# 26 products on zeros for TensorE in three of its waits at the start of a recurrent-attention and maxout kernel

## The chip, the cores and the metric

The kernel runs on one core of a Trainium2 chip. The metric is the device time in microseconds (us) of one execution; the time of a kernel is the median over its runs.

## The reference

The inputs are q, k, v and f_logit, each 4 batches x 8 heads x 768 positions x 48, and the three weight matrices of a maxout layer. All are float32, and so is the output of 3072 x 384.

```python
f = 1.0 / (1.0 + np.exp(-f_logit))
for t in range(S):
    state = f[:, :, t, :, None] * state + np.einsum('bhd,bhe->bhde', k[:, :, t], v[:, :, t])
    y[:, :, t] = np.einsum('bhd,bhde->bhe', q[:, :, t], state)
x = y.transpose(0, 2, 1, 3).reshape(B * S, H * D)
h1, h2 = x @ w1, x @ w2
out = np.maximum(h1, h2) @ w_out
```

## The kernel before

The 768 positions of each of the 4 batches are cut into windows of 256, so that there are 12 units of work, numbered 0 to 11 (unit s is window s // 4 of batch s % 4). The positions of a window are taken in chunks, and the recurrence becomes a few products per chunk. The maxout layer is rewritten: max(h1, h2) is h2 plus the ReLU of x @ (w1 - w2), so the kernel first makes the difference of the two weight matrices and the product of w2 and w_out, and then needs one wide product, one ReLU and one product with w_out for each unit.

The order of all work is written out by hand in a string, ORDER. Each word is a step: letters for the kind, the unit, for some steps a part, the engine (a = ScalarE, v = VectorE, p = GpSimd, s = SyncE) and after @ a slot of the input buffer or a bank of PSUM. An engine runs its own steps in the order in which they stand in the string; waits between engines are put in by the framework from the buffers that the steps read and write. All loads and nearly all stores go through the one DMA queue of SyncE.

The steps of the opening that matter here:

- Lf, Lk, Lq, Lv load a unit's f_logit, k, q and v into slots of one large buffer (line 115); Wa, Wb and Wo load w1, w2 (line 125) and w_out (line 129), in halves.
- E, F, G (lines 246, 250, 254) take exponentials and a logarithm of f_logit on ScalarE; e (line 257) adds two of its rows.
- C (lines 261 and 264) is the running sum over the chunk as a product with a triangular matrix, u_inc; X and Z (lines 271 and 276) take its exponentials.
- i, j, K, Q (lines 280 to 294) scale k and q; V casts v.
- t and u (line 320) transpose k and q on TensorE; U copies the transposes out of PSUM (tile trs).
- D (line 401) adds up the new state; n and N scale it. A (line 337) is the product of queries and keys, m (line 345) its mask, S (line 367) the part from the state before, y (line 387) the product with the values. z reads a word of a PSUM bank, H and Y (line 433) gather the result as xT.
- wc, wt, wx cast, transpose and store w2; ws (line 536) subtracts w2 from w1, wp (line 544) permutes the difference, we stores it; wo casts w_out, and wm (line 528) multiplies the two, wn stores that.
- d (line 445), r (line 452), o (lines 460 and 463), b and O are the layer itself: the wide product, its ReLU, the last product, the copy out of PSUM and the store.

TensorE's own order at the start is C0, t0, D0, u0, the two parts of A0, S0, C1, then products for the weights, y0 and the first d0. PSUM has eight banks; bank 7 is first used by the weight step wt1.

Of the kernel before, what the change touches and what calls it, by code (L numbers as in the profile page):

```python
# [12 lines left out]
BF16 = mybir.dt.bfloat16  # L13
# [4 lines left out]


ORDER = """  # L20
Lf0s@12 Lk0s@13 Lq0s@14 Lv0s@15 E0a Wb0s F0a Lf1s@12 G0a i0v Wb1s e0v C0@0 Wa0s X0a Wa1s Z0a K0v
V0p j0v t0@0 Lq1s@13 D0@2 Q0v Lv1s@15 n0.0v u0@0 E1a n0.1v U0v@0 F1a e1p A0.0@0 wc1a A0.1@2
m0.0v@0 S0@4 G1a Lk1s@12 wc0a C1@6 z0v@4 wt1@7 ws1v wc2a m0.1v@2 wp1@0 wx1a@7 ws3v y0 Z1a Wo0s
ws0v we1a@0 wp3@2 H0a@4 ws2v wt2@7 we3a@2 Wo1s wp0@0 j1v X1a wp2@2 Y0v@4 Q1p we0a@0 Lf2s@0 wt0@6
wx2a@7 we2v@2 d0.0@0 d0.1@1 i1v V1a K1v d0.2@2 Lf4s@13 r0.0a@0 u1@4 wx0v@6 t1@4 wo1p d0.3@3 U1v@4
wo0p D1@0 r0.1a@2 Lq2s@9 n1.0v A1.0@6 A1.1@4 wo3a wo2v S1@2 n1.1v Lk2s@10 m1.0v@6 wm0@0 E2a z1v@2
m1.1v@4 Lv2s@11 wm2@1 F2a E4a e2p y1 Lk4s@0 F4a C2@4 H1v@2 wm1@5 Y1v@2 Z2a e4p G2a Lq4s@13 wn0a@0
C4@6 X2a d1.0@2 i2v wn2a@1 j2v wn1a@5 d1.1@3 Lf3s@8 Z4a Q2v d1.2@0 X4a G4a K2v d1.3@1 V2a Lf5s@9
u2@4 t2@4 r1.1a@0 i4v o0.0@6 U2v@4 K4p Lv4s@11 r1.0a@2 j4v A2.0@0 b0.0a@6 Lq3s@10 D2@2 N1.1p
o0.1@4 n2.0v E3a m2.0v@0 Q4p Lv3s@0 F3a n2.1v S2@0 b0.1a@4 A2.1@2 z2v@0 E5a t4@6 N0.1p m2.1v@2  # L30
Lk3s@13 u4@6 N2.1p o1.0@5 F5a U4v@6 V4a Lf6s@9 e5v G5a y2 j3v b1.0a@5 D4@2 A4.0@6 H2a@0 O0s n4.0v
o1.1@5 m4.0v@6 N4.0p Lk5s@11 V3a e3p Lv5s@8 n4.1v G3a Y2v@0 C5@6 b1.1a@5 C3@7 i3p X5a S4@2 Z3a
A4.1@4 Lq5s@0 z4v@2 d2.0@0 Z5a Q3v X3a d2.1@1 E6a K3v d2.2@6 r2.0a@0 m4.1v@4 d2.3@7 Lq6s@13 t3@0
r2.1a@6 u3@0 i5p y4 D3@4 U3a@0 Lk6s@9 H4v@2 K5p o2.0@6 n3.0v Y4v@2 Lf8s@10 F6a n3.1v S3@0 b2.0v@6
A3.0@2 e6p A3.1@4 m3.0v@2 d4.0@6 Lf7s@11 N4.1p d4.1@7 j5v V5p d4.2@2 z3v@0 r4.0a@6 Lk8s@12 m3.1v@4
d4.3@3 G6a D5@6 Q5v r4.1a@2 y3 O1s C6@5 j6v H3a@0 o2.1@4 Lv6s@0 Z6a i6v E8a Y3v@0 Lq8s@8 X6a F8a
t5@2 N3.1v u5@2 b2.1v@4 Lv7s@10 d3.0@0 U5a@2 e8v d3.1@1 n5.0v Q6v d3.2@4 K6v E7a d3.3@5 Lq7s@13
C8@2 N5.0v r3.1a@4 o4.0@3 r3.0v@0 V6p F7a Lf10s@9 n5.1v G8a e7v N5.1p D6@0 Z8a A5.0@4 b4.0v@3 X8a
t6@6 Lf9s@0 j8v u6@6 C7@2 U6a@6 n6.0v o3.0@3 m5.0v@4 N6.0p Lk7s@11 V7p n6.1v X7a i8v A5.1@0
b3.0a@3 A6.0@6 S5@4 Lf11s@10 j7v Z7a K8p o3.1@3 z5v@4 m5.1v@0 Lq9s@15 m6.0v@6 y5 S6@0 Q8v H5a@4  # L40
Lv8s@12 A6.1@6 G7a o4.1@2 E9a z6v@0 i7p m6.1v@6 F9a Y5v@4 b3.1a@3 y6 e9p E10a O3s t8@6 u8@6 K7p
H6a@0 d5.0@3 Lk9s@9 U8v@6 G9a Lq10s@0 b4.1a@2 C9@5 d5.1@4 X9a O4s Y6v@0 Z9a N6.1p d5.2@6 r5.0a@3
O2s d5.3@7 Q7v d6.0@0 r5.1a@6 Lk11s@11 j9v A8.0@2 Lq11s@13 Q9p D7@4 V8a m8.0v@2 u7@6 t7@6 d6.1@1
U7a@6 n7.0v Lv9s@12 d6.2@2 N7.0v n7.1v d6.3@3 j10v E11a o5.0@4 r6.0v@0 r6.1a@2 N7.1v A7.0@0
Lv11s@10 b5.0a@4 D8@2 A7.1@6 F11a n8.0v S7@4 m7.0v@0 o6.0@3 F10a e11p Lk10s@15 G10a z7v@4 N8.0p
m7.1v@6 e10p C11@0 Lv10s@8 b6.0a@3 S8@1 i9v A8.1@6 V9p o5.1@3 z8v@1 m8.1v@6 K9v C10@6 y7 Z10a
b5.1v@3 D9@7 j11v H7a@4 y8 O5s Z11a Y7v@4 o6.1@3 X11a Q11p H8a@1 n9.0v Y8v@1 d7.0@4 b6.1a@3 i10p
G11a d7.1@5 O6s i11v d8.0@0 r7.0a@4 Q10v d8.1@1 N9.0v X10a d8.2@2 V10a K10v d8.3@3 r8.0a@0 K11v
d7.2@4 d7.3@5 r8.1v@2 u10@6 r7.1a@4 t9@0 u9@0 t10@6 t11@2 U9a@0 U10v@6 u11@2 o8.0@4 U11v@2 A9.0@0
b8.0a@4 S9@2 m9.0v@0 A9.1@6 D10@4 o7.1@5 z9v@2 m9.1v@6 V11v A11.0@0 y9 n10.0v D11@6 o7.0@4 n11.0v  # L50
m11.0v@0 N11.0p H9v@2 o8.1@0 b7.0v@4 N10.0v b7.1a@5 Y9v@2 O7s A10.0@6 b8.1a@0 S10@4 m10.0v@6
A10.1@2 d9.0@0 z10v@4 d9.1@1 m10.1v@2 d9.2@6 r9.0a@0 d9.3@7 A11.1@0 r9.1a@6 S11@2 y10 z11v@2
m11.1v@0 o9.0@6 H10a@4 Y10v@4 y11 b9.0a@6 d10.0@0 H11v@2 d10.1@1 d10.2@4 r10.0v@0 o9.1@6 Y11v@2
d10.3@5 d11.0@0 r10.1a@4 d11.1@1 b9.1a@6 d11.2@2 O9s d11.3@3 O8s o10.0@4 r11.1v@2 r11.0v@0 o10.1@3
o11.0@0 b10.0a@4 b10.1a@3 O10s P11.0@1 b11.0a@0 O11s P11.1@0 B11.0v@1 R11.0s B11.1a@0 R11.1s
"""


@with_exitstack
def kernel(  # L60
# [14 lines left out]
    nc = tc.nc  # L75
    B, H, S, D = q.shape
    C = 128
    HC = C // 2
    W = 2 * C
    nw = S // W  # L80
    NP = H // 2
# [8 lines left out]
    consts = ctx.enter_context(tc.tile_pool(name="consts", bufs=1))  # L90
    inp = ctx.enter_context(tc.tile_pool(name="inp", bufs=1))
    work = ctx.enter_context(tc.tile_pool(name="work", bufs=2))
# [16 lines left out]
    loaded = {s: {} for s in range(n_s)}  # L109
    sources = {"f": f_logit, "k": k, "q": q, "v": v}  # L110

    def load(nm, s, slot):
        w, b = divmod(s, B)
        src = sources[nm][b, :, w * W:(w + 1) * W, :].rearrange("h (p two) d -> p h (two d)", two=2)
        nc.sync.dma_start(out=slots[:, slot, :].rearrange("p (h x) -> p h x", h=H), in_=src)
        loaded[s][nm] = slots[:, slot, :].rearrange("p (h two d) -> p h two d", h=H, two=2)

    def staged(i, a):
        return slots[:, 4 * i:4 * i + 4, :].rearrange("p s x -> p (s x)").rearrange("p (a x) -> p a x", a=a)
# [10 lines left out]
                             in_=moe_w_out.rearrange("(j p) m -> p j m", p=C)[:, part, :])  # L130


    tri = consts.tile([C, 2, HC], BF16, name="tri")
    nc.gpsimd.memset(tri, 0.0)
    for h in range(2):
# [27 lines left out]
    def pad(nm, s):  # L163
        if s not in holders[nm]:
            holders[nm].append(s)
        return padded[nm][holders[nm].index(s) % len(padded[nm])]
# [157 lines left out]
    def step_U(s, e, b):  # L324
        t = work.tile([C, 2, 2, NP, 2, HC], BF16, name="trs", tag="trs", bufs=3)
        copy(e, t.rearrange("p h x j a t -> p h (x j a t)"), banks16[:, b:b + 2, :])
        tr[s] = t

    def step_A(s, jj, b):
        t = tr[s]  # L330
        for j in range(2 * jj, 2 * jj + 2):
            for par in range(2):
                for h in range(2):
                    for r in range(2):
                        rows = slice(r * DP, r * DP + D)
                        ps = banks[:, b + r, :].rearrange("p (j a t) -> p j a t", j=2, a=2)
                        nc.tensor.matmul(out=ps[h * HC:(h + 1) * HC, j % 2, par, :],  # L337
                                         lhsT=t[rows, h, 0, j, par, :],
                                         rhs=t[rows, h, 1, j].rearrange("p a t -> p (a t)"),
                                         start=True, stop=True, skip_group_check=True)  # L340

    def step_m(s, jj, b):
        if jj == 0:
            at[s] = work.tile([C, 2, 2, 2, 2, C], BF16, name="at_m", tag="at_m", bufs=2)
        nc.vector.tensor_mul(at[s][:, jj].rearrange("p r j a t -> p (r j) (a t)"),  # L345
                             banks[:, b:b + 2, :].rearrange("p r (j x) -> p (r j) x", j=2),
                             mask_f.unsqueeze(1).to_broadcast([C, 4, 2 * C]))
# [9 lines left out]
    def step_S(s, b):  # L357
        t = tr[s]
        ys[s] = [banks[:, b + h, :].rearrange("p (j t) -> p j t", j=NP) for h in range(2)]
        for h in range(2):  # L360
            if not has_state(s, h):
                continue
            st = state_before(s, h)
            for j in range(NP):
                for r in range(2):
                    rows = slice(r * DP, r * DP + D)
                    nc.tensor.matmul(  # L367
                        out=ys[s][h][r * DP:(r + 1) * DP, j, :], lhsT=st[rows, j, :],
                        rhs=t[rows, h, 1, j].rearrange("p a t -> p (a t)"),
                        start=(j == 0), stop=False, skip_group_check=True)  # L370


# [176 lines left out]
    def store_wd(part, e, b):  # L549
        n = d_ff // 4  # L550
        ps = banks[:, b:b + 2, :].rearrange("p b x -> p (b x)")[:, 0:KT * n]
        copy(e, wd[:, :, part * n:(part + 1) * n], ps.rearrange("p (k x) -> p k x", k=KT))

    steps = {
        "Lf": lambda s, e, b: load("f", s, b), "Lk": lambda s, e, b: load("k", s, b),
        "Lq": lambda s, e, b: load("q", s, b), "Lv": lambda s, e, b: load("v", s, b),
        "Wa": lambda i, e, b: load_columns(w1_f, moe_w1, e, i),
        "Wb": lambda i, e, b: load_columns(w2_f, moe_w2, e, i),
        "Wo": lambda h, e, b: load_wo(e, h),
# [5 lines left out]
        "V": lambda s, e, b: step_V(s, e),  # L565
        "t": lambda s, e, b: transposes(s, 0, b), "u": lambda s, e, b: transposes(s, 1, b),
        "U": lambda s, e, b: step_U(s, e, b),
        "A": lambda s, i, e, b: step_A(s, i, b), "m": lambda s, i, e, b: step_m(s, i, b),
        "S": lambda s, e, b: step_S(s, b), "y": lambda s, e, b: step_y(s),
        "z": lambda s, e, b: step_z(s, b),  # L570
# [10 lines left out]
        "ws": lambda i, e, b: subtract(i, e), "wp": lambda i, e, b: permuted(i, b),  # L581
        "we": lambda i, e, b: store_wd(i, e, b),
    }
    for word in ORDER.split():
        key, of, e, b = re.fullmatch(r"([A-Za-z]+)([0-9.]+)([avps]?)@?([0-9]*)", word).groups()
        steps[key](*map(int, of.split(".")), e, int(b or 0))


# [28 lines left out]
```

## Time and profile before

| | |
|---|---|
| median of 3 runs | 141.44 us (141.24 to 141.84) |
| the profiled execution, its own time | 142.99 us |
| its span, first to last instruction | 141.2 us |
| TensorE products busy | 120.8 us (86% of the span), 2331 instructions |
| VectorE busy | 110.4 us (78%) |
| ScalarE busy | 87.2 us (62%) |
| GpSimd busy | 47.7 us (34%) |
| SyncE's DMA queue | 28.22 MB, 80.9% of what 16 DMA engines could be busy in the span |

How to read it: times in the profile count from the start of the span, 1.8 us of the profiled execution lie around it. PE is TensorE's products, PEld its loading of the stationary operand, DVE VectorE, ACT ScalarE, POOL GpSimd, SPq SyncE's DMA queue. In a row of the timeline stand the start, the time that the merged instructions took, the engine, the line, the operation, what is written and read, how many there are, and in brackets how long the engine had been idle and what ended that. Products overlap in TensorE's pipeline, so the duration of one is longer than the distance between two. A row of the chain of waits has the start, the length, and the engine or transfer that held the chain.

### The profile page before, as it was taken

How to read it: one execution, taken by the hardware profiler on the slowest of the kernel's cores; microseconds unless marked ns; L12 is line 12 of the kernel's file. 1: busy time of each engine (PE TensorE's matmuls, PEld its weight loads, DVE VectorE, ACT ScalarE, POOL GpSimd, SP SyncE). 2: the span in 40 equal slices, each digit the busy share in tenths (PEclk: the TensorE clock that was granted, in tenths of full speed). 3: DMA queues.
4: the chain of work that ended last, by engine and by line, in shares of the span. 5: the costliest groups of instructions: out<-in, count | busy, mean ns of one | idle time of the engine just before them, and what ended most of it. 6: DMA issues, size and time to landing. Idle time of an engine off the chain costs nothing.

```text
span 141.2 us, 5372 instructions
## 1 busy us (share of the span) xinstructions
PE 120.8 (86%) x2331; PEld 89.9 (64%) x2331; DVE 110.4 (78%) x196; ACT 87.2 (62%) x145; POOL 47.7 (34%) x68
## 2 busy tenths in 40 slices
PE   0033899896999999999699999997999999999990
PEld 0022678653866786868466787675886668678570
DVE  5766799896879997999989898899688895770610
ACT  3624899559988899499683999715785114303120
POOL 7443205405194536800582943459100000000000
PEclk9999999999999999999999999999999999999999
DMA  4999999999999998997999999999410012000854
GB/s 114 269 331 348 382 278 300 341 236 265 264 262 269 278 276 212 248 230 185 272 265 250 233 256 271 271 271 238 101 25 5 5 34 77 5 0 16 214 125 98
DMA packets 56248, 28.66 MB, mean 203 GB/s; under 512 B 50464, under 2 KB 54688, under 8 KB 56224
## 3 DMA queue, kind: packets, MB, share of 16 engines
q1 hardware_dynamic: 56064, 28.22, 80.9%
q8 instruction: 18, 0.29, 0.9%
q10 hardware_dynamic: 160, 0.10, 0.3%
q14 instruction: 6, 0.05, 0.1%
HBM read 23.59 MB, written 4.72 MB: 200 GB/s over the span
## 4 chain that ended last, share of the span: by engine, by line
PE 57%; DMA 20%; DVE 7%; issue 5%; ACT 4%; POOL 3%; SPq 1%; ACTq 0%; DVEq 0%; POOLq 0%
PE banks L445 17%; PE banks L463 17%; DMA slots<-in_f_logit_dram 8%; PE banks L460 7%; DMA slots<-in_k_dram 6%; DMA slots<-in_moe_w_dram 6%; PE banks L337 3%; PE banks L320 3%; PE banks L387 3%; PE banks L367 2%; DVE kp L291 2%; POOL vb L104 2%; PE banks L401 2%; ACT gate L246 1%; POOL wo L104 1%
## 5 line engine op out<-in xcount | busy, mean ns | idle before, releaser
L445 PE MATMUL banks<-xT,wd 128*128 128x256 bf16 x288 | 33.7, 273 | 0.0
L463 PE MATMUL banks<-wo,gT 128*128 128x384 bf16 x184 | 33.7, 326 | 0.0
L345 DVE TENSOR_TENSOR at_m<-banks,mask 128x1024 bf16<-128x1024 f32 x24 | 29.0, 1215 | 1.7 <-PE banks L337 1.2
L445 PEld LDWEIGHTS <-wd 128*128 128x128 bf16 x288 | 27.3, 98 | 3.9
L452 ACT ACTIVATE gT<-banks 128x1024 bf16<-128x1024 f32 x18 | 18.4, 1032 | 11.8 <-PE banks L445 11.6
L463 PEld LDWEIGHTS <-gT 128*128 128x128 bf16 x184 | 18.0, 98 | 11.9
L104 ACT COPY ob<-banks 128x384 f32<-128x384 f32 (+1 forms) x19 | 8.9, 468 | 19.9 <-PE banks L463 14.8
L433 DVE SCALAR_TENSOR_TENSOR xT<-tail,gaps,banks 128x256 bf16<-128x256 bf16 x36 | 15.1, 472 | 0.1
L460 PE MATMUL banks<-m,xT 128*128 128x384 bf16 x69 | 15.1, 328 | 0.0
L246 ACT ACTIVATE gate<-slots 128x768 f32<-128x768 f32 x12 | 10.1, 846 | 7.2 <-DMA slots<-in_f_logit_dram 7.2
L104 POOL CAST vb<-slots 128x384 bf16<-128x384 f32 (+2 forms) x15 | 9.3, 657 | 13.8 <-DVE gT L454 8.3
L257 POOL TENSOR_TENSOR e<-ell 128x384 bf16<-128x384 f32 x8 | 8.0, 1001 | 13.5 <-ACT ell L250 13.5
L418 POOL TENSOR_TENSOR state<-tmp_s,dec 128x256 bf16<-128x256 f32 x10 | 6.5, 651 | 17.9 <-DVE tmp_s L413 17.9
L337 PE MATMUL banks<-trs 48*64 48x128 bf16 x384 | 10.5, 227 | 1.9 <-DVE trs L104 1.9
L261 PE MATMUL banks<-e,u_inc 128*128 128x384 bf16 x12 | 4.3, 354 | 9.2 <-DVE e L257 7.8
L454 DVE TENSOR_SCALAR gT<-banks 128x1024 bf16<-128x1024 f32 x6 | 7.2, 1218 | 4.3 <-PE banks L445 4.3
L337 PEld LDWEIGHTS <-trs 48*64 48x64 bf16 x384 | 7.5, 110 | 4.5 <-DVE trs L104 2.2
L104 ACT COPY trs<-banks 128x2048 bf16<-128x2048 bf16 x5 | 9.3, 1861 | 1.6 <-PE banks L320 1.6
L250 ACT ACTIVATE ell<-gate 128x768 f32<-128x768 f32 x12 | 10.0, 844 | 0.4
L294 POOL TENSOR_TENSOR qp<-slots,dec 128x768 bf16<-128x768 f32 x4 | 7.3, 1819 | 8.7 <-DVE slots L284 6.8
L104 DVE COPY trs<-banks 128x2048 bf16<-128x2048 bf16 x7 | 8.4, 1217 | 1.5 <-PE banks L320 1.5
L291 DVE TENSOR_TENSOR kp<-slots,inv 128x768 bf16<-128x768 f32 x8 | 7.5, 952 | 1.4 <-ACT inv L271 1.2
(73 smaller groups left out, 195.3 us busy)
## 6 DMA issues: line engine op xcount, KB each, us to landing
slots<-in_f_logit_dram SPq DMA_DIRECT2D x12, 384.0 KB, 6.4
slots<-in_k_dram SPq DMA_DIRECT2D x12, 384.0 KB, 5.7
slots<-in_q_dram SPq DMA_DIRECT2D x12, 384.0 KB, 6.0
slots<-in_v_dram SPq DMA_DIRECT2D x12, 384.0 KB, 5.9
out_dram<-ob SPq DMA_DIRECT2D x22, 192.0 KB, 3.5
slots<-in_moe_w_dram SPq DMA_DIRECT2D x4, 768.0 KB, 8.4
slots<-in_moe_w_out_dram SPq DMA_DIRECT2D x2, 768.0 KB, 7.4
out_dram<-ob SPq DMA_DIRECT2D x2, 96.0 KB, 2.2
```

Source lines behind the costliest of these rows:

```text
L104: (nc.scalar.copy if e == "a" else engines[e].tensor_copy)(out, in_)
L246: nc.scalar.activation(flat(gate[s]), flat(loaded[s]["f"]), AF.Exp, bias=0.0, scale=-1.0)
L250: nc.scalar.activation(flat(ell[s]), flat(gate[s]), AF.Ln, bias=1.0, scale=1.0)
L257: engines[e].tensor_add(pad("e", s)[:, :, 0:D], ell[s][:, :, 0, :], ell[s][:, :, 1, :])
L291: engines[e].tensor_mul(pad("kp", s)[:, :, :, 0:D], by_parity(loaded[s]["k"]), both(inv[s]))
L337: nc.tensor.matmul(out=ps[h * HC:(h + 1) * HC, j % 2, par, :], lhsT=t[rows, h, 0, j, par, :], rhs=t[rows, h, 1, j].rearrange("p a t -> p ( ...
L345: nc.vector.tensor_mul(at[s][:, jj].rearrange("p r j a t -> p (r j) (a t)"), banks[:, b:b + 2, :].rearrange("p r (j x) -> p (r j) x", j=2) ...
L433: engines[e].scalar_tensor_tensor(out=x[:, kt], in0=tails[s], scalar=gaps[:, kt:kt + 1], in1=ps[:, :, kt], op0=ALU.mult, op1=ALU.add)
L445: nc.tensor.matmul(out=ps[:, f, :], lhsT=wd[:, kt, ff * C:(ff + 1) * C], rhs=xT[g][:, kt, :], start=(kt == 0), stop=(kt == KT - 1))
L452: nc.scalar.activation(dst, src, AF.Relu)
L460: nc.tensor.matmul(out=ps, lhsT=xT[g][:, kt, cols], rhs=m2[:, kt, :], start=(kt == 0), stop=False)
L463: nc.tensor.matmul(out=ps, lhsT=gT[g][:, ff, cols], rhs=wo[:, ff, :], start=False, stop=(ff == FG - 1))
```

## The change

A tile of zeros, 128 x 512 in bf16, is set once by VectorE, ahead of its other work. A new step, J, issues a number of products of this tile with itself (a stationary operand of 128 x 128 zeros, a moving operand of 128 x 512 zeros) into PSUM bank 7. Nothing reads their result. Fifteen stand ahead of C0, six between C0 and t0, and five between u0 and A0. No step of the string is moved, removed or given to another engine.

The diff also has code that nothing calls: an empty string FIRST for loads ahead of everything, a step T that the string does not name, and an engine argument for loads, which is SyncE everywhere as before. The view of the transposed tile has its axes in another order, with the same addresses behind it.

```diff
 ORDER = """
-Lf0s@12 Lk0s@13 Lq0s@14 Lv0s@15 E0a Wb0s F0a Lf1s@12 G0a i0v Wb1s e0v C0@0 Wa0s X0a Wa1s Z0a K0v
-V0p j0v t0@0 Lq1s@13 D0@2 Q0v Lv1s@15 n0.0v u0@0 E1a n0.1v U0v@0 F1a e1p A0.0@0 wc1a A0.1@2
+Lf0s@12 Lk0s@13 Lq0s@14 Lv0s@15 J15@7 E0a Wb0s F0a Lf1s@12 G0a i0v Wb1s e0v C0@0 J6@7 Wa0s X0a
+Wa1s Z0a K0v V0p j0v t0@0 Lq1s@13 D0@2 Q0v Lv1s@15 n0.0v u0@0 J5@7 E1a n0.1v U0v@0 F1a e1p A0.0@0
...
+    idle = consts.tile([C, 512], BF16, name="idle")
+    nc.vector.memset(idle, 0.0)
     tri = consts.tile([C, 2, HC], BF16, name="tri")
...
-        tr[s] = t
+        tr[s] = t.rearrange("p h x j a t -> p x h j a t")
...
-                                         lhsT=t[rows, h, 0, j, par, :],
-                                         rhs=t[rows, h, 1, j].rearrange("p a t -> p (a t)"),
+                                         lhsT=t[rows, 0, h, j, par, :],
+                                         rhs=t[rows, 1, h, j],
...
+    def step_J(n, b):
+        for _ in range(n):
+            nc.tensor.matmul(out=banks[:, b, :], lhsT=idle[:, 0:C], rhs=idle, start=True, stop=True)
...
+        "J": lambda n, e, b: step_J(n, b),
```

More of the change, by code (lines that the diff above doesn't have):

```diff
@@ L20 @@
 ORDER = """
-Lf0s@12 Lk0s@13 Lq0s@14 Lv0s@15 E0a Wb0s F0a Lf1s@12 G0a i0v Wb1s e0v C0@0 Wa0s X0a Wa1s Z0a K0v
-V0p j0v t0@0 Lq1s@13 D0@2 Q0v Lv1s@15 n0.0v u0@0 E1a n0.1v U0v@0 F1a e1p A0.0@0 wc1a A0.1@2
[L23 to L55, printed above, removed]
-"""
+Lf0s@12 Lk0s@13 Lq0s@14 Lv0s@15 J15@7 E0a Wb0s F0a Lf1s@12 G0a i0v Wb1s e0v C0@0 J6@7 Wa0s X0a
@@ new lines @@
+Wa1s Z0a K0v V0p j0v t0@0 Lq1s@13 D0@2 Q0v Lv1s@15 n0.0v u0@0 J5@7 E1a n0.1v U0v@0 F1a e1p A0.0@0
+wc1a A0.1@2 m0.0v@0 S0@4 G1a Lk1s@12 wc0a C1@6 z0v@4 wt1@7 ws1v wc2a m0.1v@2 wp1@0 wx1a@7 ws3v y0
+Z1a Wo0s ws0v we1a@0 wp3@2 H0a@4 ws2v wt2@7 we3a@2 Wo1s wp0@0 j1v X1a wp2@2 Y0v@4 Q1p we0a@0
+Lf2s@0 wt0@6 wx2a@7 we2v@2 d0.0@0 d0.1@1 i1v V1a K1v d0.2@2 Lf4s@13 r0.0a@0 u1@4 wx0v@6 t1@4 wo1p
+d0.3@3 U1v@4 wo0p D1@0 r0.1a@2 Lq2s@9 n1.0v A1.0@6 A1.1@4 wo3a wo2v S1@2 n1.1v Lk2s@10 m1.0v@6
+wm0@0 E2a z1v@2 m1.1v@4 Lv2s@11 wm2@1 F2a E4a e2p y1 Lk4s@0 F4a C2@4 H1v@2 wm1@5 Y1v@2 Z2a e4p G2a
@@ new lines @@
+Lq4s@13 wn0a@0 C4@6 X2a d1.0@2 i2v wn2a@1 j2v wn1a@5 d1.1@3 Lf3s@8 Z4a Q2v d1.2@0 X4a G4a K2v
+d1.3@1 V2a Lf5s@9 u2@4 t2@4 r1.1a@0 i4v o0.0@6 U2v@4 K4p Lv4s@11 r1.0a@2 j4v A2.0@0 b0.0a@6
+Lq3s@10 D2@2 N1.1p o0.1@4 n2.0v E3a m2.0v@0 Q4p Lv3s@0 F3a n2.1v S2@0 b0.1a@4 A2.1@2 z2v@0 E5a
+t4@6 N0.1p m2.1v@2 Lk3s@13 u4@6 N2.1p o1.0@5 F5a U4v@6 V4a Lf6s@9 e5v G5a y2 j3v b1.0a@5 D4@2
+A4.0@6 H2a@0 O0s n4.0v o1.1@5 m4.0v@6 N4.0p Lk5s@11 V3a e3p Lv5s@8 n4.1v G3a Y2v@0 C5@6 b1.1a@5
+C3@7 i3p X5a S4@2 Z3a A4.1@4 Lq5s@0 z4v@2 d2.0@0 Z5a Q3v X3a d2.1@1 E6a K3v d2.2@6 r2.0a@0 m4.1v@4
@@ new lines @@
+d2.3@7 Lq6s@13 t3@0 r2.1a@6 u3@0 i5p y4 D3@4 U3a@0 Lk6s@9 H4v@2 K5p o2.0@6 n3.0v Y4v@2 Lf8s@10 F6a
+n3.1v S3@0 b2.0v@6 A3.0@2 e6p A3.1@4 m3.0v@2 d4.0@6 Lf7s@11 N4.1p d4.1@7 j5v V5p d4.2@2 z3v@0
+r4.0a@6 Lk8s@12 m3.1v@4 d4.3@3 G6a D5@6 Q5v r4.1a@2 y3 O1s C6@5 j6v H3a@0 o2.1@4 Lv6s@0 Z6a i6v
+E8a Y3v@0 Lq8s@8 X6a F8a t5@2 N3.1v u5@2 b2.1v@4 Lv7s@10 d3.0@0 U5a@2 e8v d3.1@1 n5.0v Q6v d3.2@4
+K6v E7a d3.3@5 Lq7s@13 C8@2 N5.0v r3.1a@4 o4.0@3 r3.0v@0 V6p F7a Lf10s@9 n5.1v G8a e7v N5.1p D6@0
+Z8a A5.0@4 b4.0v@3 X8a t6@6 Lf9s@0 j8v u6@6 C7@2 U6a@6 n6.0v o3.0@3 m5.0v@4 N6.0p Lk7s@11 V7p
@@ new lines @@
+n6.1v X7a i8v A5.1@0 b3.0a@3 A6.0@6 S5@4 Lf11s@10 j7v Z7a K8p o3.1@3 z5v@4 m5.1v@0 Lq9s@15 m6.0v@6
+y5 S6@0 Q8v H5a@4 Lv8s@12 A6.1@6 G7a o4.1@2 E9a z6v@0 i7p m6.1v@6 F9a Y5v@4 b3.1a@3 y6 e9p E10a
+O3s t8@6 u8@6 K7p H6a@0 d5.0@3 Lk9s@9 U8v@6 G9a Lq10s@0 b4.1a@2 C9@5 d5.1@4 X9a O4s Y6v@0 Z9a
+N6.1p d5.2@6 r5.0a@3 O2s d5.3@7 Q7v d6.0@0 r5.1a@6 Lk11s@11 j9v A8.0@2 Lq11s@13 Q9p D7@4 V8a
+m8.0v@2 u7@6 t7@6 d6.1@1 U7a@6 n7.0v Lv9s@12 d6.2@2 N7.0v n7.1v d6.3@3 j10v E11a o5.0@4 r6.0v@0
+r6.1a@2 N7.1v A7.0@0 Lv11s@10 b5.0a@4 D8@2 A7.1@6 F11a n8.0v S7@4 m7.0v@0 o6.0@3 F10a e11p
@@ new lines @@
+Lk10s@15 G10a z7v@4 N8.0p m7.1v@6 e10p C11@0 Lv10s@8 b6.0a@3 S8@1 i9v A8.1@6 V9p o5.1@3 z8v@1
+m8.1v@6 K9v C10@6 y7 Z10a b5.1v@3 D9@7 j11v H7a@4 y8 O5s Z11a Y7v@4 o6.1@3 X11a Q11p H8a@1 n9.0v
+Y8v@1 d7.0@4 b6.1a@3 i10p G11a d7.1@5 O6s i11v d8.0@0 r7.0a@4 Q10v d8.1@1 N9.0v X10a d8.2@2 V10a
+K10v d8.3@3 r8.0a@0 K11v d7.2@4 d7.3@5 r8.1v@2 u10@6 r7.1a@4 t9@0 u9@0 t10@6 t11@2 U9a@0 U10v@6
+u11@2 o8.0@4 U11v@2 A9.0@0 b8.0a@4 S9@2 m9.0v@0 A9.1@6 D10@4 o7.1@5 z9v@2 m9.1v@6 V11v A11.0@0 y9
+n10.0v D11@6 o7.0@4 n11.0v m11.0v@0 N11.0p H9v@2 o8.1@0 b7.0v@4 N10.0v b7.1a@5 Y9v@2 O7s A10.0@6
@@ new lines, with words @@
+b8.1a@0 S10@4 m10.0v@6 A10.1@2 d9.0@0 z10v@4 d9.1@1 m10.1v@2 d9.2@6 r9.0a@0 d9.3@7 A11.1@0 r9.1a@6
+S11@2 y10 z11v@2 m11.1v@0 o9.0@6 H10a@4 Y10v@4 y11 b9.0a@6 d10.0@0 H11v@2 d10.1@1 d10.2@4 r10.0v@0
+o9.1@6 Y11v@2 d10.3@5 d11.0@0 r10.1a@4 d11.1@1 b9.1a@6 d11.2@2 O9s d11.3@3 O8s o10.0@4 r11.1v@2
+r11.0v@0 o10.1@3 o11.0@0 b10.0a@4 b10.1a@3 O10s P11.0@1 b11.0a@0 O11s P11.1@0 B11.0v@1 R11.0s
+B11.1a@0 R11.1s
+"""
+FIRST = ""
+def words(order):
+    for word in order.split():
+        key, of, e, b = re.fullmatch(r"([A-Za-z]+)([0-9.]+)([avps]?)@?([0-9]*)", word).groups()
+        yield key, tuple(map(int, of.split("."))), e, int(b or 0)
@@ L110, with load @@
     sources = {"f": f_logit, "k": k, "q": q, "v": v}
-    def load(nm, s, slot):
+    def load(nm, s, e, slot):
         w, b = divmod(s, B)
         src = sources[nm][b, :, w * W:(w + 1) * W, :].rearrange("h (p two) d -> p h (two d)", two=2)
-        nc.sync.dma_start(out=slots[:, slot, :].rearrange("p (h x) -> p h x", h=H), in_=src)
+        engines[e].dma_start(out=slots[:, slot, :].rearrange("p (h x) -> p h x", h=H), in_=src)
         loaded[s][nm] = slots[:, slot, :].rearrange("p (h two d) -> p h two d", h=H, two=2)
+    for key, of, e, b in words(FIRST):
+        load(key[1], *of, e, b)
     def staged(i, a):
@@ L326, in step_U, with step_T @@
         copy(e, t.rearrange("p h x j a t -> p h (x j a t)"), banks16[:, b:b + 2, :])
-        tr[s] = t
+        tr[s] = t.rearrange("p h x j a t -> p x h j a t")
+    def step_T(s, x, e):
+        if s not in tr:
+            t = work.tile([C, 2, 2, NP, 2, HC], BF16, name="trs", tag="trs", bufs=3)
+            tr[s] = t.rearrange("p h x j a t -> p (h x j a t)").rearrange(
+                "p (x a j h t) -> p x h j a t", x=2, a=2, j=NP, h=2)
+        out = tr[s][:, x].rearrange("p h j a t -> p a j h t").rearrange("p a j h t -> p (a j) (h t)")
+        engines[e].dma_start_transpose(
+            out=out, in_=pad("kpqp"[2 * x:2 * x + 2], s).rearrange("p two h e -> p (two h e)"))
     def step_A(s, jj, b):
@@ L368, in step_S @@
                         out=ys[s][h][r * DP:(r + 1) * DP, j, :], lhsT=st[rows, j, :],
-                        rhs=t[rows, h, 1, j].rearrange("p a t -> p (a t)"),
+                        rhs=t[rows, 1, h, j],
                         start=(j == 0), stop=False, skip_group_check=True)
@@ L552, in store_wd @@
         copy(e, wd[:, :, part * n:(part + 1) * n], ps.rearrange("p (k x) -> p k x", k=KT))
+    def step_J(n, b):
+        for _ in range(n):
+            nc.tensor.matmul(out=banks[:, b, :], lhsT=idle[:, 0:C], rhs=idle, start=True, stop=True)
     steps = {
-        "Lf": lambda s, e, b: load("f", s, b), "Lk": lambda s, e, b: load("k", s, b),
-        "Lq": lambda s, e, b: load("q", s, b), "Lv": lambda s, e, b: load("v", s, b),
+        "J": lambda n, e, b: step_J(n, b),
+        "Lf": lambda s, e, b: load("f", s, e, b), "Lk": lambda s, e, b: load("k", s, e, b),
+        "Lq": lambda s, e, b: load("q", s, e, b), "Lv": lambda s, e, b: load("v", s, e, b),
         "Wa": lambda i, e, b: load_columns(w1_f, moe_w1, e, i),
@@ L567 @@
         "U": lambda s, e, b: step_U(s, e, b),
+        "T": lambda s, x, e, b: step_T(s, x, e),
         "A": lambda s, i, e, b: step_A(s, i, b), "m": lambda s, i, e, b: step_m(s, i, b),
@@ L583 @@
     }
-    for word in ORDER.split():
-        key, of, e, b = re.fullmatch(r"([A-Za-z]+)([0-9.]+)([avps]?)@?([0-9]*)", word).groups()
-        steps[key](*map(int, of.split(".")), e, int(b or 0))
+    for key, of, e, b in words(ORDER):
+        steps[key](*of, e, b)
 _INS = ['q', 'k', 'v', 'f_logit', 'moe_w1', 'moe_w2', 'moe_w_out']
```

## The prediction

> **What bounds the kernel now.** I read the slices of the page first. The two rows below share the span out in 40 slices of 3.5 us; a digit is the busy share in tenths.
>
> ```profile
> PE   0033899896999999999699999997999999999990
> ...
> DMA  4999999999999998997999999999410012000854
> ```
>
> The DMA engines are busy from the second slice to the 28th, about 100 us. TensorE is idle for two slices, partly busy up to some 35 us, and then nearly full to the end. So two things can set the end: the loads, and TensorE from about 35 us on. A change in the opening counts only if it moves the moment from which TensorE is full.
>
> The timeline of TensorE's products over the first 36 us shows the three waits that the change fills, and that moment.
>
> ```profile
> 7.79 0.48 PE L261 MATMUL banks<-e,u_inc 128*128 128x384 bf16 x1 [7.79 <-DVE e L257]
> 8.06 0.29 PE L264 MATMUL banks<-ones,e 128*128 128x2 bf16 x4
> 9.93 0.61 PE L320 MATMUL banks<-ident,kp 64*128 64x64 bf16 x16 [1.58 <-DVE kp L291]
> 11.92 0.65 PE L401 MATMUL banks<-vb,kp 64*64 64x64 bf16 x32 [1.38 <-POOL vb L104]
> 12.50 0.61 PE L320 MATMUL banks<-ident,qp 64*128 64x64 bf16 x16
> 14.74 1.07 PE L337 MATMUL banks<-trs 48*64 48x128 bf16 x32 [1.64 <-DVE trs L104]
> ...
> 33.32 0.32 PE L261 MATMUL banks<-e,u_inc 128*128 128x384 bf16 x1 [1.37 <-POOL e L257]
> ```
>
> J15 goes ahead of the first row, J6 between C0 (7.79, 8.06) and t0 (9.93), J5 between u0 (12.50) and A0 (14.74). The last row is C2. TensorE stood idle for 1.37 us before it; the stage table has it busy for 26.68 of the 26.70 us that follow, and the chain of waits stays on it to 53 us. So C2 is the moment. The timeline of all engines shows what holds it:
>
> ```profile
> 26.15 1.60 POOL L104 CAST wo<-slots 128x768 bf16<-128x768 f32 x2 [2.34 <-DMA slots<-in_moe_w_out_dram]
> ...
> 30.48 0.84 ACT L246 ACTIVATE gate<-slots 128x768 f32<-128x768 f32 x1 [1.39 <-DMA slots<-in_f_logit_dram]
> 31.36 0.84 ACT L250 ACTIVATE ell<-gate 128x768 f32<-128x768 f32 x1
> ...
> 32.28 0.99 POOL L257 TENSOR_TENSOR e<-ell 128x384 bf16<-128x384 f32 x1 [4.53 <-ACT ell L250]
> ```
>
> E2, F2, e2 and C2 follow one another with no slack, and E2 waited 1.39 us for its load, f2. C2 is set by a transfer, and the steps ahead of it hang on transfers too. The chain of waits, with start and length, has
>
> ```profile
> 6.28 8.15 DMA slots<-in_moe_w_dram
> ...
> 15.12 8.84 DMA slots<-in_k_dram
> ```
>
> which land at 14.43 (wc1 at 14.51 waits for it) and 23.96 (i1 at 23.98). In the trace's landing records the halves of w1 arrive at 16.45 and 18.55, q1 at 21.20, those of w_out at 26.09 and 28.24, f2 at 30.41: one stream with no hole. VectorE's ws1, ws3, j1 and i1 start at 16.64, 18.64, 21.30 and 23.98, close behind.
>
> **What the Trainium skill says.** "TensorE: Matmul & The Clock Gate", Part 1: TensorE's clock is halved until it has been busy for a window of about 3.4 us, and the window is free-running. The trace agrees on the size: 16 transposes take 0.61 us at 9.93 and 12.50, but 0.41 at 24.92; the permuting products (L544) fall from 421 to 273 ns within the group at 17.64. So the opening runs at half clock to about 18.4 us. No sentence of the page says that zeros count less for this gate than other data, and no run yet shows it. The same page, Part 2, has weight loads pulled ahead of products in flight: the trace shows u_inc loaded at 1.99 for a product at 7.79, and 0.77 us of loads inside the 1.01 us of wt1. "VectorE: DVE Perf Modes", "Zero memsets can be issued as uint32 (trn2)", halves the elements of the new memset; the trace agrees, with uint32 rows for bf16 tiles (L155 and L158).
>
> **The change part by part.**
>
> *The memset.* Four rows of 528 words take 2.17 us (L155), 0.54 each, so 256 words are some 0.26 us, at the head of VectorE's queue. Queued behind it are the memsets and copies of u_inc. The first copy waits 0.34 us for GpSimd's tri, and before i0 VectorE waits 0.82 us for ScalarE's exponential of the load f0. Cost 0; were it 0.53, the 0.82 would still cover it.
>
> *One J.* At full clock, 256 columns (L445, 18 in 2.17 us, one of them 0.27) are 0.112 us apart, 384 columns (L528, 16 in 2.77, one of them 0.33) 0.163. So 128 columns are 0.051, and 512 are 0.214; at half clock twice that, 0.43. Weight loads of 0.10 us hide behind them.
>
> *J15.* VectorE starts at 0.82; with the memset the zeros are there at about 1.1. All at half clock end at 1.15 + 15 x 0.43 = 7.6, ahead of e0's 7.79. If a full window lifts the clock, which can be at 4.6 to 8.0 by its phase, the end is as early as 1.15 + 8 x 0.43 + 7 x 0.214 = 6.1. Cost 0, with a pipeline's tail of 0.1 at worst.
>
> *J6.* C0 would end near 8.2 at full clock; 6 x 0.214 = 1.3 gives 9.5, ahead of t0's 9.9. At half clock 8.4 + 2.6 = 11.0, and t0 is 1.1 late, but D0 behind it waits for GpSimd's V0 until 11.92, so that nothing passes on. Cost 0.
>
> *J5.* At full clock u0 ends near 12.9, and 1.1 more is 14.0, ahead of A0's 14.7. At half clock it is 13.1 + 2.15 = 15.25, and A0 is 0.5 late. What waits is the mask m0, VectorE's whole queue behind it, and S0, C1 and the weight steps on TensorE. C2's 1.37 us of idle time covers that, and VectorE's wait of 0.47 us for w_out at 28.26 takes up most of it there.
>
> *The gain.* At full clock, row by row: C0 -0.16, t0, D0 and u0 -0.20 each, A0 -0.43, S0 -0.25, C1 -0.15, wt1 -0.40, the first seven L544 products -0.36: 2.35 us of TensorE's time. On a path lie only C0 (X0 waits for it), D0 (the update of the state waits 0.9 us for it) and the first half of A0 (m0 waits 0.74 us): 0.16, and 0.2 + 0.2 after V0 has set D0. So VectorE leads by 0.4 at 15.4 us. Then ws1 cannot start before 16.45, ws3 not before 18.55 (a lead of 0.09), i1 not before 23.96 (0.02). TensorE's lead, up to 2 us, becomes a longer wait before C2. No load moves: v1, k1, w_out and f2 are issued behind V0, E1 and one another, and though q1 is issued after K0 at 9.90, and could go 0.16 sooner, it stands behind the weights, the last of which lands at 18.55.
>
> *The sum.* 0 - 0 = 0 on the profiled execution of 142.99 us, whose span is 141.2. That execution is 1.55 above the median of 141.44; the difference carries over, so 141.4.
>
> **The rivals.**
>
> *A lead gets through (faster).* If C2 hung on something other than f2, or the loads came sooner with the steps that free their slots, VectorE's 0.4 us up to half of TensorE's 2 us could arrive, most likely 0.9: 140.5. The steps' starts at 16.64 to 30.48, each within 0.2 us of a landing, speak against it.
>
> *Each J serial with its weight load, and the clock stays at half (slower).* A J then costs 0.43 + 0.10 = 0.53. J15 ends at 9.1, C0 at 9.7, J6 at 12.9, t0, D0 and u0 at 14.7, J5 at 17.4; A0 is 2.65 late. Less the 1.37 before C2 that is 1.3: 142.7. It decides once A0 is over 1.4 us late. Weight loads overlapping products in the same stretch (wt1, above) speak against it.
>
> *Zeros do not lift the clock.* All costs then stand at their half-clock values, A0 is 0.5 late, the 1.37 us covers it: 141.4 as well. Only the rows would tell.
>
> **How the numbers follow.** No change 0.81 (zeros that leave the clock at half included), a lead that gets through 0.10, serial products or another delay of A0 beyond the slack 0.09. About 0.5%, 0.7 us, is what a measurement of this kernel can tell from no change; the three runs of before lie within 0.6. The likeliest case covers 140.9 to 141.9, with that spread and 0.1 for C0; the range reaches into both others, to 140.7 and 142.1.
>
> **What would show it.** Right: 26 products of 128x512, about 0.43 us apart and later 0.21; transposes of t0 and u0 at 0.41 us instead of 0.61; A0 no later than 14.7; E2 at 30.5 and C2 at 33.3 as before, with 2 to 3 us of idle time before it instead of 1.37. Wrong on the bound: E2 or the landing of f2 over 0.5 us earlier, and TensorE full from then. Wrong on the cost: C0 after 8.0, or A0 after 16.1.

## The result, and the profile after

In the comparison made with the prediction the changed kernel took 143.16 us (median of 4 executions, 143.0 to 143.94) against 141.34 (4, 141.2 to 141.84): slower by a ratio of 1.0126, 95% interval 1.0083 to 1.0169. Two longer comparisons gave less: 141.97 against 141.73 (16 and 59 executions, ratio 1.0022, 0.9998 to 1.0047), and 142.27 against 141.66 (22 and 67, 1.0045, 1.0017 to 1.0072). The ratios leave out executions over 1.5% above the fastest of their kernel (up to 11 of 23 in the kernels below), the medians here and below do not. So there is a loss, of 0.2 to 0.6 us in the medians of the longer comparisons, the smaller of which does not exclude no loss in its ratio; why the first one had 1.8 is not settled.

The profiled execution took 143.94 us, with a span of 142.2. Its slices of the page, with the granted clock, are

```profile
PE   6755569989999999999999999999999999999990
...
PEclk9999955999999999999999999999999999999998
DMA  4999999995999999999999799999520013000844
```

TensorE is busy from the start, as it should be, but the clock is at half in slices 6 and 7 (18 to 25 us), and the DMA engines have a hole in slice 10. The timeline of TensorE's products shows what happened:

```profile
1.19 5.08 PE L582 MATMUL banks<-idle 128*128 128x512 bf16 x15 [1.19 <-DVE idle L148]
7.76 0.32 PE L277 MATMUL banks<-e,u_inc 128*128 128x384 bf16 x1 [1.49 <-DVE e L273]
...
8.02 1.46 PE L582 MATMUL banks<-idle 128*128 128x512 bf16 x6
9.73 0.41 PE L336 MATMUL banks<-ident,kp 64*128 64x64 bf16 x16 [0.26 <-DVE kp L307]
...
14.36 0.64 PE L363 MATMUL banks<-trs 48*64 48x128 bf16 x32 [0.67 <-DVE trs L114]
...
15.59 0.62 PE L538 MATMUL banks<-ident,w2b 128*128 128x128 bf16 x8
18.97 1.65 PE L570 MATMUL banks<-wdn,perm 128*128 128x256 bf16 x7 [2.76 <-DVE wdn L562]
...
23.02 1.06 PE L538 MATMUL banks<-ident,w2b 128*128 128x128 bf16 x8
...
35.42 0.34 PE L277 MATMUL banks<-e,u_inc 128*128 128x384 bf16 x1
```

Up to 16.2 us all goes as forecast: J15 ends at 6.3 and J6 at 9.5, the clock rises at 4.6 us, the transposes take 0.41, C0 is at 7.76 and A0 at 14.36. Then TensorE waits 2.76 us ahead of wp1 for the difference w1 - w2, and from 18.3 to 25.1 us it is back at half clock (wt2, at 23.02, takes 1.06 us; wt1 took 0.62). In the kernel before, wt2 ran at full clock:

```profile
20.40 0.61 PE L512 MATMUL banks<-ident,w2b 128*128 128x128 bf16 x8
```

C2 comes at 35.42 instead of 33.32, with no idle time ahead of it. VectorE and SyncE's queue in the same stretch, before and after:

```profile
15.12 3.29 SPq L115 DMA_DIRECT2D slots<-in_k_dram  x1
...
16.64 0.95 DVE L536 TENSOR_TENSOR wdn<-slots 128x768 bf16<-128x768 f32 x1
...
18.46 2.55 SPq L129 DMA_DIRECT2D slots<-in_moe_w_out_dram  x1
```

```profile
15.51 4.15 SPq L125 DMA_DIRECT2D slots<-in_k_dram  x1
...
17.96 0.96 DVE L562 TENSOR_TENSOR wdn<-slots 128x768 bf16<-128x768 f32 x1 [1.84 <-DMA slots<-in_moe_w_dram]
...
19.70 1.38 SPq L142 DMA_DIRECT2D slots<-in_moe_w_out_dram  x1
```

ws1 waited for the first half of w1 (Wa0), which landed at 17.87; before it was 16.45. The issue of k1 took 4.15 us (before 3.29), and w_out was issued at 19.70 (before 18.46). So a load was late although no load was moved. The view of the DMA queues in the window from 15 to 18 us shows what is new in it:

```profile
q1 hardware_dynamic: 759, 1.11, 103.0%
q8 instruction: 1, 0.02, 2.3%
```

(packets, the single pieces that a transfer is cut into; MB; share of the 16 engines). The same window of the kernel before has no packet on queue 8; it has one in the window from 18 to 21. The DMA records give it as one packet of 16,384 bytes, started at 15.69 us after the change and at 18.78 before, that holds one DMA engine for 1.13 and 1.26 us. The page counts 18 such packets, 0.29 MB. The Trainium skill, "Perfetto Trace Analysis" (The 4-stage abstract model), has instructions of 64 bytes; by that figure I estimate TensorE's 2331 products and 2331 weight loads at 298 KB, and the 18 packets are 295 KB, so this queue most likely carries TensorE's own program. By the same estimate 26 products more, with their weight loads, are 3.3 KB of it ahead of the same work. The packet is called the fetch below.

### The profile page after: what moved, and what is told of

Same layout as the page of the kernel before. It is cut to its first block, busy times and chain, and to the rows that moved or that the text cites. A ratio compares the mean times of both kernels' runs of the same rounds, so it can differ in the third digit from the quotient of the medians.

```text
span 142.2 us, 5424 instructions
## 1 busy us (share of the span) xinstructions
PE 129.0 (91%) x2356; PEld 92.5 (65%) x2357; DVE 110.6 (78%) x197; ACT 87.2 (61%) x145; POOL 48.5 (34%) x68
## 4 chain that ended last, share of the span: by engine, by line
PE 74%; DMA 10%; DVE 6%; issue 3%; ACT 2%; SPq 1%; POOL 1%; ACTq 0%; DVEq 0%
PE banks L471 21%; PE banks L489 19%; PE banks L486 8%; DMA slots<-in_moe_w_dram 7%; PE banks L413 4%; PE banks L336 4%; PE banks L363 4%; PE banks L570 3%; PE banks L554 3%; PE banks L393 3%; DMA slots<-in_f_logit_dram 3%; PE banks L427 2%; PE banks L277 1%; DVE kp L307 1%; SPq L138 1%
## 5 line engine op out<-in xcount | busy, mean ns | idle before, releaser
L478 ACT ACTIVATE gT<-banks 128x1024 bf16<-128x1024 f32 x18 | 18.4, 1031 | 12.6 <-PE banks L471 12.4
L114 ACT COPY ob<-banks 128x384 f32<-128x384 f32 (+1 forms) x19 | 8.9, 467 | 19.8 <-PE banks L489 14.7
L262 ACT ACTIVATE gate<-slots 128x768 f32<-128x768 f32 x12 | 10.2, 847 | 5.7 <-DMA slots<-in_f_logit_dram 5.7
L307 DVE TENSOR_TENSOR kp<-slots,inv 128x768 bf16<-128x768 f32 x8 | 8.0, 1006 | 1.2 <-ACT inv L287 1.0
L307 POOL TENSOR_TENSOR kp<-slots,inv 128x768 bf16<-128x768 f32 x4 | 7.5, 1865 | 4.2 <-DVE slots L296 4.1
```

What stands on the lines that cost most here:

```text
L114: (nc.scalar.copy if e == "a" else engines[e].tensor_copy)(out, in_)
L262: nc.scalar.activation(flat(gate[s]), flat(loaded[s]["f"]), AF.Exp, bias=0.0, scale=-1.0)
L307: engines[e].tensor_mul(pad("kp", s)[:, :, :, 0:D], by_parity(loaded[s]["k"]), both(inv[s]))
L478: nc.scalar.activation(dst, src, AF.Relu)
```

## The experiments

Medians of each kernel and of the kernel before beside it, the ratio, and from each one's profiled execution the start of that packet, the length of k1's issue and the start of C2, in us:

| kernel | median, before | ratio (95%) | packet | k1 issue | C2 |
|---|---|---|---|---|---|
| b_again | 141.36, 141.73 | 0.9967 (0.9946-0.9989) | 19.20 | 3.29 | 32.74 |
| memset_only | 141.59, 141.73 | 0.9989 (0.9966-1.0012) | 19.09 | 3.29 | 32.54 |
| tiny10 | 141.56, 141.76 | 0.9995 (0.9976-1.0014) | 19.02 | 3.28 | 33.30 |
| j15_only | 141.75, 141.76 | 1.0004 (0.9977-1.0030) | 18.75 | 3.29 | 33.38 |
| warm_late | 141.75, 141.66 | 0.9997 (0.9967-1.0027) | 18.55 | 3.29 | 32.69 |
| cold_late | 141.74, 141.66 | 1.0000 (0.9979-1.0021) | 19.07 | 3.29 | 32.69 |
| tiny26 | 142.37, 141.73 | 1.0026 (1.0001-1.0051) | 15.90 | 4.14 | 33.39 |
| tiny52 | 142.43, 141.76 | 1.0020 (0.9994-1.0046) | 15.84 | 4.15 | 34.95 |
| a_again | 141.97, 141.73 | 1.0022 (0.9998-1.0047) | 15.98 | 4.14 | 35.86 |
| a_third | 142.27, 141.66 | 1.0045 (1.0017-1.0072) | 15.92 | 4.14 | 33.54 |
| hold | 141.83, 141.66 | 1.0001 (0.9977-1.0024) | 15.93 | 4.14 | 33.79 |

b_again is the kernel before itself; its interval misses 1, so a single ratio within some 0.3% of 1 tells little, and only that of a_third is farther off. What the rows have is agreement: each with the packet at 15.8 to 16.0 us has a higher median than each with it at 18.55 to 19.20, if by only 0.08 us at the closest.

**The two kernels again** (no edit).

> The kernel before, unchanged, for more of its executions and a second profile. Its first profiled execution took 142.99 us where the others took 141.2 to 141.8. If the place of the rise of TensorE's clock makes that difference (it rose at 18.4 us in the first profile[...]), a second profile should have the rise elsewhere and a C2 some 1.5 us earlier than 33.3. Fetch theory (below, tiny26): the 16 KB packet of TensorE's instructions is at about 18.8 us again, and Wa0 lands at about 16.4. Time 141.3 to 141.5.

> The changed kernel, unchanged, for a second profile. In the first one TensorE's second fetch of instructions (16 KB, one packet of 1.1 us on one DMA engine) went at 15.7 us instead of 18.8, the first half of w1 (Wa0) landed at 17.87 instead of 16.45, and the clock fell to half from 18.3 to 25.1. Fetch theory: the packet is at 15.7 again, and Wa0 lands after 17.5. Clock theory: the fall to half is there again, and its length goes with the time. Time 143.0 to 143.3 in either case.

> The changed kernel once more, since its loss came out as 1.3% in the first comparison and as 0.2% in the second. Fetch theory: the 16 KB packet at 15.6 to 16.0 us in any execution, w1 late by over 1 us, a loss of 0.2 to 0.5% in the median, and single executions up to 2% longer where the clock falls back for two windows. Rival (the first comparison's 1.3% is the size): again over 1%.

The first repetition of the changed kernel came out a microsecond under what I expected of it, at 141.97. The packet is at 15.9 to 16.0 us in both repetitions of the changed kernel, and at 19.20 in that of the kernel before. The second profile of the kernel before has its clock rise at 19.0 us, later than the first one's 18.4, and yet takes 140.71 us instead of 142.99: the phase of the clock was not the difference, and that guess fell. In the timeline of b_again, C2 is the row

```profile
32.74 0.32 PE L261 MATMUL banks<-e,u_inc 128*128 128x384 bf16 x1 [0.62 <-POOL e L257]
```

an idle time of 0.62 us ahead of it instead of 1.37. Of the seven profiles with a late packet, the one that the prediction was read from has the longest idle time there; the others have from none (cold_late) to 1.18 us (tiny10).

The fall back to half clock differs between executions: in a_again from 18.7 to 25.5 us, in a_third not at that place (there w1's first half landed at 16.54, and its second at 19.75). Of the 43 executions of the changed kernel, 11 have a mean clock of 0.976 or less, which is some 7 us or more at half; they took 142.4 to 144.8 us, median 143.7. The other 32 have a median of 142.05. That is a correlation: a late w1 could bring the fall and the longer time alike.

**The same instructions without the work.**

```diff
-            nc.tensor.matmul(out=banks[:, b, :], lhsT=idle[:, 0:C], rhs=idle, start=True, stop=True)
+            nc.tensor.matmul(out=banks[:, b, 0:2], lhsT=idle[:, 0:C], rhs=idle[:, 0:2], start=True, stop=True)
```

> The changed kernel with the moving operand of its 26 products on zeros cut from 512 columns to 2: the same number of instructions for TensorE ahead of the weight steps, next to no work in them. Fetch theory (26 products more bring TensorE's second fetch of instructions forward onto the first half of w1): the packet at 15 to 16 us, Wa0 after 17.5, and most of the loss stays: 142.5 to 143.3. Clock theory (the loss is the fall back to half clock after an early rise): no early rise, so no fall, and 141.2 to 141.6.

No early rise of the clock (18.9 us), and still a median 0.6 us above that of the kernel before. The packet is at 15.90 and k1's issue as long as in the changed kernel, but here it was the second half of w1 that came late (19.81; 18.55 before), so that the fourth quarter of the difference (ws3) and wp3 waited, as rows of its timeline show:

```profile
19.84 1.83 DVE L562 TENSOR_TENSOR wdn<-slots 128x768 bf16<-128x768 f32 x2 [1.25 <-DMA slots<-in_moe_w_dram]
...
20.85 0.38 PE L570 MATMUL banks<-wdn,perm 128*128 128x256 bf16 x2 [1.20 <-DVE wdn L562]
```

So neither the zeros' time nor an early clock is needed: 26 more products with next to no work in that place are enough for a median of this size.

**The memset alone** (J15, J6 and J5 taken out of ORDER).

> The changed kernel without any of the 26 products: the memset of the tile of zeros, its 1 KB per partition in SBUF and the other code stay. Fetch and clock theories: as the kernel before, 141.2 to 141.6. If the memset or the shifted addresses cost something, slower than that by its price.

Nothing is lost that this comparison can tell: memset, SBUF addresses and unused code are free within 0.3%.

**The fetch put back, with and without the early clock.**

```diff
         src = pad("kpqp"[2 * x:2 * x + 2], s)
+        if s == 0:
+            for h in range(2):
+                nc.tensor.matmul(out=banks[:, b + h, :], lhsT=idle[:, 0:C], rhs=idle, start=True, stop=True)
+            return
```

(cold_late has the cut of tiny26 as well.)

> The changed kernel with its 26 products on zeros, but the 32 transposes of unit 0 (t0 and u0) are replaced by 4 products on zeros that fill the same two banks, so that unit 0's queries and keys are left out of the computation. TensorE then has 28 products fewer ahead of the weight steps, two fewer than the kernel before. Fetch theory: the 16 KB packet goes back to 18 to 20 us, Wa0 lands at about 16.4, TensorE waits under 1.5 us ahead of the first permuting product, the clock stays at full, and the loss goes: 141.0 to 141.6. Clock theory (an early rise by itself brings the fall back): the fall near 18 us stays, and over 141.9 with it.

> The same replacement of t0 and u0, with the 26 products cut to 2 columns: the control of warm_late, with the place of the fetch as before and no early rise of the clock. Fetch theory: the packet at 18 to 20 us, Wa0 at 16.4, C2 at 32.5 to 33.3, 141.2 to 141.7, so some 0.5 below tiny26. If the early clock is worth something once the fetch is out of the way, warm_late is below this one; by my prediction's own reading (loads set C2) the two are equal within 0.3.

Both kernels leave unit 0's queries and keys out, and both give the time of the kernel before. In warm_late the clock rises at 6.7 us and stays up, Wa0 lands at 16.75, and the timelines of SyncE's queue and of TensorE have

```profile
15.34 3.29 SPq L125 DMA_DIRECT2D slots<-in_k_dram  x1
```

```profile
17.85 0.92 PE L574 MATMUL banks<-wdn,perm 128*128 128x256 bf16 x7 [1.33 <-DVE wdn L566]
...
32.69 0.32 PE L277 MATMUL banks<-e,u_inc 128*128 128x384 bf16 x1 [0.68 <-POOL e L273]
```

k1's issue is back at 3.29, and C2 is at 32.69 in both kernels. All 26 products run, and cost nothing once the fetch is late: that speaks for the place of the fetch. It is not a clean proof, since the two kernels also give TensorE less to do ahead of A0, but where the fetch now falls can be read: of the 16 parts in which each load reports its landing, q1, behind w1, has 15 by 20.27 us in warm_late and the last at 21.30. And full clock from 6.7 us on instead of 21.4 gains nothing: TensorE waits for w1 and f2 with it as without.

**The wait filled.**

```diff
-... m0.1v@2 wp1@0
+... m0.1v@2 J6@0 wp1@0
```

> The changed kernel with six more products on zeros ahead of the first permuting product (wp1), where TensorE waited 2.8 us for the late half of w1. The fetch stays at 15.6 to 16.0 us and w1 stays late. Clock theory: with that window filled the clock stays at full from its rise on, the permuting products run 0.11 us apart instead of 0.22, C2 comes 1.5 to 2 us sooner than the changed kernel's 35.4, and the time is 141.2 to 141.6. Fetch theory alone: what is left of the loss is w1's lateness, 141.6 to 142.0. If the six end after w1's difference is ready, they add their own 0.1 to 0.3.

The fetch is at 15.93 and w1's second half is late (19.78), but TensorE is busy ahead of wp1, and the clock, at full from 15.2 us, does not fall at 18. One of 22 executions has a mean clock of 0.976 or less, where the changed kernel had 11 of 43. Its median, 141.83, is the lowest of those with an early fetch, and still not below the kernel before. C2, at 33.79, came 1.6 us sooner than in the changed kernel's first profile, but that is not shown to be the filling: w1's first half was on time here (16.44), and in a_third, where it was on time too and nothing was filled, C2 came at 33.54.

**How far the fetch moves.** j15_only takes J6 and J5 out of the changed kernel; the other two change the counts of tiny26.

```diff
-J15@7 ... J6@7 ... J5@7
+J10@7                      (tiny10)
+J41@7 ... J6@7 ... J5@7    (tiny52)
```

> The changed kernel with the first 15 products alone (J6 and J5 taken out). The fetch follows the count of TensorE's products: about 130 had been issued at 18.8 to 19.2 us in the kernel before, and 15 more ahead put it at about 17 us. Fetch theory: packet at 16.5 to 17.5, and k1's issue on SyncE's queue between the 3.29 us of a late fetch and the 4.14 of the fetch at 15.9; E2 at 29.9 to 30.7, 141.5 to 142.1. Clock theory: the clock rises at 4.6 to 8.0 and falls back once TensorE idles between C0 and D0, so that the opening runs at half clock again: no gain and no loss, 141.3 to 141.7.

> Ten products of 2 columns ahead of C0 and no others: a smaller step in the place of the fetch, with no work for the clock. Fetch theory: packet at about 17 to 18 us, k1's issue 3.3 to 3.9 us, E2 at 29.7 to 30.4, time between memset_only's 141.6 and tiny26's 142.3. Rival (a step, not a slope: only the count over some limit matters): either exactly as memset_only or exactly as tiny26.

> Twice the products of 2 columns (41, 6 and 5). Their own time is 41 x 0.1 = 4 us ahead of C0, inside the wait of 7.8. Fetch theory: the packet goes to 14.5 to 15.2 us, while A0 is issued, and still falls on w1's first half: Wa0 or Wa1 late by about 1.1 us, k1's issue 4.1 us or more, E2 at 30.4 to 31.0, 142.0 to 142.6. If the loss grew with the number of products rather than with the fetch, it would be twice that of tiny26: 142.9 or more.

My expectation of a slope was wrong, and the rival of a step right: with 0, 10 or 15 products ahead the packet starts at 18.8 to 19.2 us, with 26 or 52 at 15.7 to 16.0, and nothing lies between. A likely reason, argued and not shown: the packet is asked for when TensorE's issue passes a point in its program, and issue itself is held up by waits, so that the point is passed at one such wait or at another (the second mask, for which y0 waits, ends at 18.72 in the kernel before, and the cast for wt1 at 15.56). In the median the loss goes with the packet: tiny52, with twice the products (its first 41 took 1.26 us, not the 4 that I expected), costs what tiny26 costs. j15_only is also the clean case on the clock: it is at half from 10.9 to 21.1 us, mean clock 0.963, and the time is that of the kernel before.

**Where the loss sits.** The medians hide how it is spread. Of the 97 executions in the five rows with an early fetch, 26 took 143 us or more (10 of 23 in tiny52, 6 of 22 in hold); of the 116 in the six rows with a late one, 4. The fall of the clock is not needed for that: five of the six in hold have a mean clock of 0.985 or more. The six profiles with an early fetch divide in the same way. In three (the changed kernel's first, a_again, tiny52) w1's first half landed at 17.87 to 18.16 us, C2 came 4.4 to 4.5 us after f2's landing, and the execution took 143.9 to 144.6 us. In the other three (a_third, tiny26, hold) the first half was on time and only the second was late, C2 came 2.9 us after f2, as it did in all seven profiles with a late fetch, and the execution took 141.6 to 141.9. f2 landed at 30.46 to 31.34 in these six, at 29.61 to 30.46 in the seven. So f2 sets C2, as predicted, unless w1's first half is late; then TensorE, behind its products for w1, does. Six profiles are few, and why the fetch delays the one half or the other is open.

## Why the prediction was wrong

**The step that failed** is in the gain: "No load moves". I took the order of SyncE's queue and the frees of its slots as all that could move a load. TensorE's own program comes through the same DMA engines as the loads; 26 products more brought a fetch of 1.1 us forward by 3 us, from the stretch of q1 onto w1. It seems to hold back the one DMA engine that carries it: 15 of the 16 parts of w1's first half were there at 16.43 us in both kernels, but the last came at 17.87 instead of 16.45, and ws1 needs all. The landings that the prediction was read from already had this mark, on q1: 15 parts by 20.01, the last at 21.21, just behind the fetch at 18.78. k1's issue grew by 0.86 us, w_out went out 1.2 later, and f2 landed at 31.03 instead of 30.41. The fetch on record does not account for all of that: v1's issue, ahead of k1's, already took 3.72 us instead of 3.13 and ended at 15.42, before the packet started at 15.69; that part is open. The products, which I had costed at 0 by their time, had a price in bytes that I had not looked for. The page had the row of that queue, and its 18 packets were in front of me. How large the loss comes out varies from one comparison to the next: the 141.97 of a_again would have lain in my range, with the same step wrong.

**The slack that was not typical.** "C2's 1.37 us of idle time covers that" held for the execution I had read, at 142.99 us. In b_again it is 0.62. It was not what failed, since A0 was on time at 14.36, but a slack read from one execution, 1.5 us above the median, was no ground for "the difference carries over".

**What the clock does after it has risen** was missing. My rivals had it rise or not rise. It rose at 4.6 us, and fell again in the wait for w1: wp1 to the start of wp2 then ran at half clock up to 25 us, where the kernel before had been at full since 18.4. In a_again and a_third it was at half already from 11.84 to 15.25 and from 12.19 to 15.60, and A0, at 15.19 and 15.01, was later than the 14.7 I had given as the limit. One execution out of four had some 7 us or more of half clock, and took 143.7 in the median, against 142.05. That the clock is what costs this is not shown: j15_only is at half for 10.2 us without a loss, and hold has its long executions without the fall.

**What held.** J15, J6 and J5 end where the sum put them, at 6.3, 9.5 and ahead of A0; the memset is free (memset_only); zeros do lift the clock, and J15's products are 0.43 us apart up to the rise and 0.22 after it; f2's landing sets C2 in ten of the 13 profiles; and a lead of TensorE in the opening is worth nothing, since loads set C2 (warm_late and cold_late, 0.9997 and 1.0000). So the mechanism that I gave for no gain was right. What was missing was the loss, which came with the slower rival's sign but not by its way: no product was serial with its weight load.

**What stays open.** The medians with the early packet (141.83 to 142.43) and with the late one (141.36 to 141.75) do not overlap, but single executions do: tiny26's profiled one took 141.62. From C2 to the end of the span the 13 profiles take 106.2 to 108.8 us, a spread as large as most differences in C2. In j15_only and tiny10 C2 was at 33.3 to 33.4 without a loss in the median; there a second packet came at 27.2 to 27.3, ahead of f2's landing at 30.4. So C2 in one profile doesn't size the loss, and the links from the late w1 to the last half microsecond at the end were not followed one by one. Nor is it settled why all five executions of the first comparison were above 142.7.

## What to carry to other kernels

Instructions are bytes that the DMA engines must bring, here 16 KB at a time: where loads are back to back and their consumers wait for each, look at the instruction queue's packets and at what they fall on before adding or removing instructions, even idle ones. In this kernel warming TensorE's clock gained nothing where loads set the end of the stretch, and once warm the clock fell back in a wait for a load. Before a slack is counted on, see whether the profiled execution is a typical one. And where a few long executions carry a loss, count them: a median shows little of it.

## What the runs showed of the hardware

- A fetch of what is most likely TensorE's program is one packet of 16 KB, 0.9 to 2.1 us long over all profiles. With the first one at 15.69 to 15.98 us, one of the 16 parts of a half of w1 landed 1.2 to 1.6 us behind the other 15.
- Products on zeros count for the clock: it rose at 4.1 to 6.7 us after a start at 1.2.
- The clock fell after windows of 3.4 us in which TensorE had been busy for 1.33 us (14.85 to 18.26, the changed kernel's first profile), 1.56 and 1.63 us (8.43 to 11.84 and 15.25 to 18.67 in a_again), and stayed at full after 1.86 and 2.30 (8.02 to 11.43 and 11.43 to 14.85, first profile). So it doesn't take an idle window. How much work is enough does not follow from the busy time alone: in warm_late the clock stayed at full after a window with 1.48 us on record (10.07 to 13.48).
